# Backward pass of an attention and FFN block: y and dx each in one pass a token tile, 64-row chunks of weight gradients as two column halves

## The chip, the cores and the metric

The kernel runs on one core of one Trainium2 chip. The metric is the device time of one execution in microseconds (us). The kernel before takes 1388.32 us, the median of three runs from 1385.99 to 1391.23.

## The reference

A transformer block with the attention and the FFN side by side, forward and backward in one launch, batch 1, 2048 tokens (S), width 448 (D), 16 heads of 28 (DH), FFN width 1792 (F), all in bf16:

```python
xn = layernorm(x)                                  # no scale, no shift
qkv = xn @ wqkv                                    # [2048, 1344]
p = softmax(q @ k.T * 28 ** -0.5)                  # a head at a time, [2048, 2048]
attn = (p @ v) @ wo
ffn = (silu(xn @ w_gate) * (xn @ w_up)) @ w_down
y = x + attn + ffn
out, vjp = jax.vjp(f, x, wqkv, wo, w_gate, w_up, w_down)
return out, *vjp(grad_out)     # y, dx, dwqkv, dwo, dw_gate, dw_up, dw_down
```

## The kernel before, in words

Token tiles are 128 tokens (16 of them), and the 16 heads go in four groups of four (`g`), two pairs to a group (`hp`). Width 448 is cut into four chunks for gradients whose rows are D (`DCH`): three of 128 rows and one, chunk 3, of 64.

**Forward pass.** For each group of heads the scores of 512 queries by 128 keys are computed, exponentiated and multiplied with V. Between these matmuls PE runs filler units in a fixed order, most of them the FFN: for each of 14 blocks of 128 FFN columns (`fc`) and each of four column chunks of 512 tokens (`sc`) the gate, up and dh products are formed, and `dh_unit` (L422) writes h, da and du for that block side by side into one tile `hda` of 128 x 3 x 512, transposes it by a DMA on the SP queue into `f_sp` (`sp_transpose`, L434 and L435), and stores it whole to DRAM (`F_d`, L436). `dw_unit` (L441) then reads `f_sp` for the weight gradients of this block, 16 matmuls over the token tiles for each of w_down, w_gate and w_up (L445). For the last block the gate and up gradients are not done here: the transposes go to DRAM (`fT_d`, L438) for the backward pass. The attention outputs in transposed form go to `OT_d` (`mid3`, L541 to L543).

**Backward pass.** A loop (L1362) runs over 512 steps k: group, pair of heads, chunk of 512 keys (`kc`), chunk of 512 queries (`qc`), token tile in it (`qi`). In each step:

- `row` (L844): two score matmuls (L852) into PSUM tiles `sb` (3 buffers) and, for the step before, two dP matmuls (L860) into `db` (3 buffers).
- `ew` (L879): two exponentials on ACT (L883), two products on DVE (L891) that give dS; dS is transposed by DMA on SP (L877), except for the last token tile of four, which PE transposes (`tr_unit`, L951, with a copy on ACT, L956). For eleven sets of four steps (`TWO`) PE transposes two tiles.

What follows depends on k mod 4:

- 0: fillers.
- 1: `kv` (L958) adds four steps to the dK and dV accumulator (L969, L973); after 16 steps ACT drains it. The row sums of dx (`aux`) are done here, save where k mod 16 is 1. `dq_unit` (L990) runs 16 matmuls of 256 columns on four column tiles of PE (L1000); ACT drains them (L1004 in the first chunk of keys, else L1013 with an add on POOL, L1015 or L1017).
- 2: fillers.
- 3: fillers, then `tr_unit`.

**Fillers** come from a list, `stream`; each is a generator that issues one matmul at a time and gives its estimated duration in ns. `fill_open` (L1302) takes the next unit, `fill_step` (L1312) issues matmuls until a budget is spent: in steps 2 and 3 of four the budgets are R2 = 560 and R3 = 380 ns; in step 0 what is left of the unit is finished, or, if none is open, a unit of up to 600 ns is opened and run. So one unit normally takes one set of four steps. All use one PSUM tile (`genb`, 1 buffer). In order:

- `late_dw`: the gate and up gradients of the last FFN block, four chunks of 16 matmuls (110 ns each), drained by DVE.
- `y_unit` (L1128): 4 chunks of 512 tokens x 2 halves of the FFN x 4 token tiles, nine matmuls of 448 columns (L1139). Half 0 is added to x by DVE into a float32 tile `yt` (L1144), half 1 is added to that by DVE and stored (L1147). Its operands, `h_c` from `F_d`, `o_c` from `OT_d` and `x_c`, are loaded for half a chunk at a time.
- `dx_open` (L1158): closes the pool of y and opens that of dx.
- `dx_unit` (L1183): three parts of the FFN blocks (`FQ`: 5, 4 and 5 of 14) x 4 chunks of 512 tokens x 4 token tiles; 10, 8 and 10 matmuls (L1195). Part 0 is copied by ACT (L1201) into the float32 array `dxg`, parts 1 and 2 are added to it by DVE (L1203). Operands: `wguT` from the transposed weights, `dau_c` (da and du) from `F_d`.
- `tail_open` (L1210), then `dc_unit` (L1242): the part of dx that comes through q, k and v, eight matmuls a token tile (L1249), an add on DVE, and POOL work on `dxg`.
- As each group of heads ends, eight-transpose units `dsp_unit` and `dsq_unit` and the dwqkv units `dwq_unit` (L1077) are put into the list: four chunks of D rows, 16 matmuls of 336 columns (L1081), four copies (L1088 to L1091) and one store each. `dsq_unit` goes in at the fourth place of the list, `dwq_unit` behind `dx_open` or `tail_open`, at the sixth place or later.

**Loads and stores.** Loads of the backward pass are queued with a due step (`drip`, L785) and issued on SP, some per step, so that each meets its date (`drop`); `have` issues at once what is still held back when its user comes. A store is held for two steps and issued by POOL, after the loop by SP (`store`, `flush`, L842).

**The end.** After step 512 the dx tiles are finished with the last group's q, k and v (`dx_mm`, `dx_a`, `dx_b`, L1358 stores dx), and the last group's `dwq_unit` chunks run with the tag "rest", which makes their copies ACT's.

Of the kernel before, what the change touches and what calls it, by code (L numbers as in the profile page):

```python
# [104 lines left out]
def kernel(  # L105
# [32 lines left out]
    OT_d = dram.tile([4, P, G, 512], BF16)  # L138
    F_d = dram.tile([4, P, NFC, 3, 512], BF16)
    fT_d = dram.tile([P, 4, 2, 4, P], BF16)  # L140
# [144 lines left out]
    def qkv_unit(g, tq, sc, act=False):  # L285
# [12 lines left out]
        else:  # L298
            if tq == 2 and sc == 0:
                if g == 0:  # L300
                    VV[g] = ff.tile([P, 4, 3, 4, P], BF16, name="f_sp")[:, 0:2].rearrange("p a w t f -> p (a w t f)")[:, :S]
# [120 lines left out]
    def dh_unit(fc, sc):  # L422
# [8 lines left out]
        DVE.scalar_tensor_tensor(out=t3[:, 2], in0=ps[:], scalar=0.5, in1=ag[:], op0=ALU.mult, op1=ALU.mult)  # L431
        DVE.scalar_tensor_tensor(out=t3[:, 1], in0=ps[:], scalar=0.5, in1=nn[:], op0=ALU.mult, op1=ALU.mult)  # L432
        if sc == 0:
            fsp[fc] = ff.tile([P, 4, 3, 4, P], BF16, name="f_sp")  # L434
        sp_transpose(fsp[fc][:, sc].rearrange("p w t f -> p (w t) f"), t3[:].rearrange("p w s -> p (w s)"))  # L435
        SP.dma_start(out=F_d[sc, :, fc], in_=t3[:])  # L436
        if fc == NFC - 1 and sc % 2:
            late.append((fT_d[:, sc - 1:sc + 1], fsp[fc][:, sc - 1:sc + 1, 1:3]))  # L438
        yield 216

    def dw_unit(fc, w):  # L441
        rhs = dy_sp if w == 0 else xn_sp
        ps = new_gen([P, 512], FP32, name="gen")
        for t in range(NT):
            PE.matmul(ps[:, :D], lhsT=fsp[fc][:, t // 4, w, t % 4, :], rhs=rhs[:, t, :],  # L445
# [81 lines left out]
    def mid3(g, qc):  # L527
# [14 lines left out]
                     (OT_d[qc, :, g, :], tT[:, 0].rearrange("p q s -> p (q s)")),  # L542
# [210 lines left out]
    yst, wdp = ExitStack(), {}  # L753

    def turn_loads():
# [3 lines left out]
        ye = yst.enter_context(tc.tile_pool(name="ye", bufs=1, side="right", reuse_waits="tile"))  # L759
        wdp[0] = ye.tile([P, 7, D], BF16, name="wd_e")  # L760
# [163 lines left out]
    fT = bk.tile([P, 4, 2, 4, P], BF16, name="dsp", bufs=1)  # L924
# [6 lines left out]
    def late_dw(c):  # L931
        d0, dn = DCH[c]
        ps = ps_g.tile([P, 2, P], FP32, name="genb")
        for t in range(NT):
            PE.matmul(ps[:dn], lhsT=xn_sp[:, t, d0:d0 + dn], rhs=fT[:, t // 4, :, t % 4, :],
                      start=(t == 0), stop=(t == NT - 1))
            if t < NT - 1:
                yield 110
        DVE.tensor_copy(out=w2[:dn, c], in_=ps[:dn])
        for a, o in enumerate((out_4, out_5)):  # L940
            store(o[d0:d0 + dn, F - P:], w2[:dn, c, a])
        yield 110
# [47 lines left out]
    def dq_unit(b):  # L990
# [27 lines left out]
        if qc == 3:  # L1018
# [5 lines left out]
            if hp == 1:  # L1024
                stream[3:3] = [(480, lambda hp=hp: dsq_unit(g, hp)) for hp in range(2)]
# [441 lines left out]
```

## Time and profile before

The profiled execution is one run of its own; the trace and the page are of it.

| | |
|---|---|
| time of the profiled execution | 1388.41 us |
| span of its trace | 1386.6 us |
| mean granted TensorE clock | 0.99 |
| bytes moved by DMA | 266.06 MB, in 664,879 packets |
| packets under 512 bytes | 590,586 |
| ACT exponentials of the backward pass (L883) | 1024, 542.0 us |
| DVE products of the backward pass (L891) | 770 + 254, 484.2 + 163.4 us |
| y matmuls (L1139), dx matmuls (L1195), dwq matmuls (L1081) | 288, 448, 256 |

How to read the profile: PE is TensorE's matmuls, PEld its weight loads, DVE VectorE, ACT ScalarE, POOL GpSimd, SP the sync engine that issues DMAs (SPq is its DMA queue). L12 is line 12 of the kernel. A group of instructions is given as line, engine, operation, out<-in with partitions x elements and type, the count (x16), then busy us, mean ns of one, and idle time before it with what ended it. A row of a window shows its bounds and length, each engine's busy time with its instructions, the granted clock, the mean share of the 16 DMA engines, and GB/s; the count may take in an instruction that lies over a window's edge. The DMA share can go over 1 where packets lie over each other. A row of the timeline shows the start, how long, engine, line, operation, out<-in, and in brackets the idle time before with what ended it; neighbouring instructions of one line are one row. A row of DMA issues gives the count, then least, mean and greatest ns of an issue.

### The profile page before, as it was taken

What the parts mean: (1) busy time and instruction counts of PE and PEld (TensorE: products, weight loads), DVE (VectorE), ACT (ScalarE), POOL (GpSimd) and SP (SyncE); (2) the same over time, 40 slices, a digit from 0 to 9 for tenths busy, and PEclk for the clock granted to TensorE, in tenths of its full rate; (3) what the DMA queues carried; (4) which work ended last, traced back from release to release, by engine and by line L of the source; (5) the groups of instructions that cost most, each with busy time, mean ns of one, the idle gap of its engine ahead of it and who ended that gap; (6) DMA issues with size and microseconds to landing.
All of it is one profiled execution on the core that took longest, in us unless ns stands there. A gap on an engine that the chain in (4) does not pass through costs nothing.

```text
span 1386.6 us, 35026 instructions
## 1 busy us (share of the span) xinstructions
PE 1321.6 (95%) x12808; PEld 563.4 (41%) x12808; DVE 1137.9 (82%) x1996; ACT 1225.6 (88%) x2242; POOL 467.3 (34%) x642
## 2 busy tenths in 40 slices
PE   5899999999999999989999999999999999999997
PEld 2333333333333333334444444444444444444443
DVE  6587666766667676759999999988899999999997
ACT  5799998989999999878899999899889898888995
POOL 6473533463344454301121211201211111114674
PEclk9899999999999999999999999999999999999999
DMA  6697968777788776789999999999999999999992
GB/s 159 150 216 174 232 132 187 180 169 159 169 176 199 161 157 157 170 246 199 219 217 217 222 232 173 213 220 223 249 188 182 196 231 233 206 189 206 209 190 67
DMA packets 664879, 266.06 MB, mean 192 GB/s; under 512 B 590586, under 2 KB 639218, under 8 KB 664706
## 3 DMA queue, kind: packets, MB, share of 16 engines
q1 hardware_dynamic: 656258, 250.59, 89.9%
q0 software_dynamic: 7040, 12.93, 4.1%
q8 instruction: 100, 1.64, 0.5%
q14 instruction: 73, 0.60, 0.1%
q10 hardware_dynamic: 1408, 0.30, 0.1%
HBM read 64.37 MB, written 59.62 MB: 89 GB/s over the span
## 4 chain that ended last, share of the span: by engine, by line
PE 79%; DVE 9%; DMA 4%; ACT 3%; issue 2%; POOL 2%; SPq 0%; ACTq 0%; DVEq 0%; POOLq 0%
PE sb L852 13%; PE acc L969 8%; PE gen L445 8%; PE genb L1195 7%; PE genb L1139 5%; PE s_w L643 4%; PE sb L951 4%; PE sb L1000 4%; PE gen L478 4%; PE gen L380 3%; PE db L860 3%; PE gen L412 3%; PE gen L292 2%; PE gen L426 2%; PE genb L1081 2%
## 5 line engine op out<-in xcount | busy, mean ns | idle before, releaser
L883 ACT ACTIVATE e_sb<-sb 128x512 bf16<-128x512 f32 x1024 | 542.0, 609 | 18.5 <-PE db L860 15.8
L891 DVE TENSOR_TENSOR ds_sb<-db,e_sb 128x512 bf16<-128x512 f32 x770 | 484.2, 682 | 30.7 <-issue 12.2
L646 ACT ACTIVATE eT<-s_w 128x1024 bf16<-128x1024 f32 x256 | 264.5, 1033 | 53.6 <-PE s_ps L643 50.8
L648 ACT ACTIVATE eT<-s_ps 128x512 bf16<-128x512 f32 x512 | 287.1, 614 | 0.0
L852 PE MATMUL sb<-kd,qd 32*128 32x512 bf16 x1024 | 235.2, 381 | 4.3 <-DMA qd<-QD_d 0.9
L860 PE MATMUL db<-kd,qd 32*128 32x512 bf16 x1024 | 230.0, 382 | 3.1 <-DVE ds_sb L891 2.5
L891 DVE TENSOR_TENSOR ds_pe<-db,e_sb 128x512 bf16<-128x512 f32 x254 | 163.4, 685 | 18.7 <-PE db L860 10.2
L1015 POOL TENSOR_TENSOR dq_acc<-dq_acc,dq_st 128x256 f32<-128x256 f32 x64 | 46.1, 720 | 389.7 <-ACT dq_st L1013 389.7
L404 POOL TENSOR_TENSOR nn<-nn,ag 128x512 f32<-128x512 f32 x56 | 71.2, 1271 | 239.6 <-DVE ag L402 238.3
L969 PE MATMUL acc<-e_sb,qd 128*32 128x512 bf16 x1024 | 134.0, 384 | 0.0
L643 PE MATMUL s_ps<-QQ,KK 32*128 32x512 bf16 x512 | 119.1, 387 | 2.2
L1195 PE MATMUL genb<-wguT,dau_c 128*128 128x448 bf16 x448 | 109.8, 356 | 0.0
L973 PE MATMUL acc<-ds_sb,qd 128*32 128x512 bf16 x770 | 106.6, 385 | 0.0
L643 PE MATMUL s_w<-QQ,KK 32*128 32x512 bf16 x512 | 100.6, 389 | 2.2 <-ACT eT L646 0.9
L852 PEld LDWEIGHTS <-qd 32*128 32x128 bf16 x1024 | 48.4, 91 | 127.6 <-issue 109.4
L956 ACT COPY dsT<-sb 128x512 f32<-128x512 f32 x144 | 84.0, 591 | 17.0 <-PE sb L951 8.6
L445 PE MATMUL gen<-xn_t,f_sp 128*128 128x448 bf16 x416 | 91.8, 354 | 0.4 <-DVE nn L419 0.3
L445 PEld LDWEIGHTS <-f_sp 128*128 128x128 bf16 x640 | 55.8, 98 | 76.4 <-issue 28.6
L1000 PE MATMUL sb<-dsT,kd 128*32 128x256 bf16 x2048 | 78.4, 273 | 2.9 <-DMA dsT<-ds_sb 2.9
L951 PE MATMUL sb<-ident_bf,ds_pe 128*128 128x128 bf16 x1016 | 77.6, 219 | 0.3
L951 PEld LDWEIGHTS <-ds_pe 128*128 128x128 bf16 x1016 | 66.1, 98 | 22.4 <-issue 5.5
L478 PE MATMUL gen<-eT,VS 128*32 128x512 bf16 x1024 | 68.6, 382 | 6.2 <-DVE hda L432 2.9
(184 smaller groups left out, 2123.2 us busy)
## 6 DMA issues: line engine op xcount, KB each, us to landing
F_d<-hda SPq DMA_DIRECT2D x56, 384.0 KB
dau_c<-F_d SPq DMA_DIRECT2D x24, 512.0 KB
qd<-QD_d SPq DMA_DIRECT2D x16, 512.0 KB
kd<-KD_d SPq DMA_DIRECT2D x16, 384.0 KB
dsT<-ds_sb SPq DMA_TRANSPOSE x367
h_c<-F_d SPq DMA_DIRECT2D x8, 512.0 KB
wT_d<-wT_f SPq DMA_DIRECT2D x14, 256.0 KB
KD_d<-qk_sp SPq DMA_DIRECT2D x7, 512.0 KB
```

The source lines that it names most:

```text
L445: PE.matmul(ps[:, :D], lhsT=fsp[fc][:, t // 4, w, t % 4, :], rhs=rhs[:, t, :], start=(t == 0), stop=(t == NT - 1))
L643: PE.matmul(sp4[hh], lhsT=KK[g][r:r + HP, kt * P:(kt + 1) * P], rhs=QQ[g][r:r + HP, qsl], start=True, stop=True, tile_position=(r, 0))
L646: ACTE.activation(out=e2[0][:], in_=wide[:], func=ACT.Exp, scale=SCALE)
L648: ACTE.activation(out=e2[1][:, j], in_=sp4[2 + j], func=ACT.Exp, scale=SCALE)
L852: PE.matmul(s_ps[:], lhsT=qside[g, qc][r:r + HP, 0, qi * P:(qi + 1) * P], rhs=kside[g, kc][r:r + HP, 0, :], start=True, stop=True, tile_po ...
L860: PE.matmul(d_ps[:], lhsT=qside[g, qc][r:r + HP, 1, qi * P:(qi + 1) * P], rhs=kside[g, kc][r:r + HP, 1, :], start=True, stop=True, tile_po ...
L883: ACTE.activation(out=est[k][:, j], in_=sps.pop((k, j))[:], func=ACT.Exp, scale=SCALE)
L891: DVE.tensor_tensor(out=ds[:, j], in0=dps.pop((k - 1, j))[:], in1=est[k - 1][:, j], op=ALU.mult)
L951: PE.transpose(ps[:, c, :], ds[:, c // 4, (c % 4) * P:(c % 4 + 1) * P], ident_bf[:])
L969: PE.matmul(a[r:r + HP, :], lhsT=sp4[:, 1, r:r + HP], rhs=e[:, j, :], start=first, stop=last, tile_position=(0, r), skip_group_check=True)
L1000: PE.matmul(ps[r:r + HP, :256], lhsT=ks[:, kt, h:h + HP], rhs=t[:, par::2, j, kt, :], start=(kt == 0), stop=(kt == 3), tile_position=(0, r ...
L1195: PE.matmul(ps[:, :D], lhsT=d[:, i // 2, i % 2, tsl], rhs=dxs["w", fq][:, i // 2, i % 2, :], start=(i == 0), stop=(i == n - 1))
```

## The change

1. **DRAM layout.** `F_d` is replaced by `H_d` (h, in eight chunks of 256 tokens) and `G_d` (da and du of one token tile side by side, in 16 token tiles). `dh_unit` writes da and du interleaved per 128 tokens and issues two stores a tile, where one was. `OT_d` is cut into eight chunks of 256 tokens. The transposed tile `f_sp` and `fT_d` hold the same blocks in the order h, then da and du of each token tile.
2. **y in one pass.** A unit is one token tile: 18 matmuls into one accumulation, one DVE add of x, one store. w_down is held whole, its pool `wr` is later reused for the weights of dx. Loads are per 256 tokens, three sets of buffers.
3. **dx in one pass.** A unit is one token tile: 28 matmuls into one accumulation, one ACT copy into `dxg`. The transposed gate and up weights are held whole, loaded in halves during y and behind `dx_open`; da and du come in three pieces a token tile, five buffers.
4. **64-row chunks.** Chunk 3 of `late_dw` and of `dwq_unit` runs as two halves of the output columns, on PE columns 0 to 63 and 64 to 127: 32 matmuls of half the columns. Its output then lies in 128 partitions: for `dwq_unit` one copy and four stores, where four copies and one store were.
5. **The filler scheduler.** Budgets are 760, 570 and 380 ns in steps 0, 2 and 3; units run over several sets of four steps; a unit is finished when what is left is within the budget and an allowance (230 ns in step 0, 700 for a dwq chunk of 128 rows, none elsewhere); the next one may open at once, but not in step 3 right after a unit ended. `dsq_unit` goes in as soon as the units of 480 ns ahead of it are through, `dwq_unit` behind it. The row sums run in any step 1.

The diff, cut to this:

```diff
@@ forward, dh_unit and dw_unit
-    F_d = dram.tile([4, P, NFC, 3, 512], BF16)
+    H_d = dram.tile([8, P, NFC, 256], BF16)
+    G_d = dram.tile([NT, P, NFC, 2, P], BF16)
...
-        DVE.scalar_tensor_tensor(out=t3[:, 2], in0=ps[:], scalar=0.5, in1=ag[:], op0=ALU.mult, op1=ALU.mult)
-        DVE.scalar_tensor_tensor(out=t3[:, 1], in0=ps[:], scalar=0.5, in1=nn[:], op0=ALU.mult, op1=ALU.mult)
+        t4 = lambda x: x.rearrange("p (t s) -> p t s", s=P)
+        dau = t3[:, 1:3].rearrange("p a s -> p (a s)").rearrange("p (t w s) -> p t w s", t=4, w=2)
+        for w, x in ((1, ag), (0, nn)):
+            DVE.scalar_tensor_tensor(out=dau[:, :, w, :], in0=t4(ps[:]), scalar=0.5, in1=t4(x[:]),
+                                     op0=ALU.mult, op1=ALU.mult)
...
-        sp_transpose(fsp[fc][:, sc].rearrange("p w t f -> p (w t) f"), t3[:].rearrange("p w s -> p (w s)"))
-        SP.dma_start(out=F_d[sc, :, fc], in_=t3[:])
+        sp_transpose(fsp[fc][:, sc], t3[:].rearrange("p w s -> p (w s)"))
+        SP.dma_start(out=H_d[2 * sc:2 * sc + 2, :, fc, :].rearrange("c p s -> p c s"),
+                     in_=t3[:, 0].rearrange("p (c s) -> p c s", c=2))
+        SP.dma_start(out=G_d[4 * sc:4 * sc + 4, :, fc].rearrange("t p w s -> p t (w s)"),
+                     in_=dau.rearrange("p t w s -> p t (w s)"))
@@ dwq_unit
+            r = dsp[g][:, t].rearrange("p k (h r) -> p (k h) r", r=HP)[:, :, :DH]
...
+                for a in range(2):
+                    PE.matmul(ps[64 * a:64 * a + 64, :6 * DH].rearrange("p (a r) -> p a r", r=DH),
+                              lhsT=xn_sp[:, t, d0:], rhs=r[:, 6 * a:6 * a + 6],
+                              start=(t == 0), stop=(t == NT - 1), tile_position=(0, 64 * a), skip_group_check=True)
...
+            cp(out=of[:, :6 * DH], in_=ps[:, :6 * DH])
+            store(w0[:, 0, g * n:(g + 1) * n], of[:64, :n])
+            store(w0[:, 1, g * n:g * n + n // 2], of[:64, n:n + n // 2])
+            store(w0[:, 2, g * n:(g + 1) * n], of[64:, :n])
+            store(w0[:, 1, g * n + n // 2:(g + 1) * n], of[64:, n:n + n // 2])
@@ y_unit
+    def y_unit(t):
+        c = t // 2
+        if t % 2 == 0:
+            have(("y", c, 0))
+            if 0 < c < 6:
+                load_y(c + 2, now + 24)
+            if c > 0:
+                load_w(0, c - 1, c, now + 16)
...
+        for i in range(NFC + G):
+            if i == NH and t % 2 == 0:
+                have(("y", c, 1))
+            l, r = (h_c[:, i, tsl], wd[:, i, :]) if i < NFC else (o_c[:, i - NFC, tsl], wo_sb[:, i - NFC, :])
+            PE.matmul(ps[:, :D], lhsT=l, rhs=r, start=(i == 0), stop=(i == NFC + G - 1))
...
+        DVE.tensor_tensor(out=y[:], in0=ps[:, :D], in1=x_c[:, t % 2, :], op=ALU.add)
+        store(out0_d[:, t, :], y[:])
@@ dx_unit
+    FP = [(0, 5), (5, 10), (10, 14)]
+    def load_dx(n, due):
+        f0, f1 = FP[n % 3]
+        dau[n] = dxs["pool"].tile([P, 5, 2, P], BF16, name="dau")
+        drip(("dx", n), [(dau[n][:, :f1 - f0], G_d[n // 3, :, f0:f1])], due)
+    def dx_unit(t):
...
+            for w in range(2):
+                PE.matmul(ps[:, :D], lhsT=dau[n][:, fc % 5, w, :], rhs=wgu[fc // NH][:, fc % NH, w, :],
+                          start=(fc + w == 0), stop=(fc + w == NFC))
...
+        ACTE.copy(out=dxs["g"][:, t, :], in_=ps[:, :D])
@@ the scheduler
+    R0, R2, R3 = 760, 570, 380
...
+    def fill_step(ns, over=0):
+        nonlocal cur, left, ended
+        if now == ended + 1 and now % 4 == 3:
             return
+        if 0 < left <= ns + over:
+            ns = left + 95
+        n = 0
+        while ns > 95:
+            if cur is None:
+                if n == 0:
+                    fill_open()
+                if cur is None:
+                    return
+            x = next(cur)
+            ns -= x
+            left -= x
+            n += 1
+            if left < 50:
+                run(cur)
+                cur, ended = None, now
...
-            if 9 <= k < NB and cur is None:
-                fill_open(600)
-            fill_step(100 if 18 < k < 36 else BIG)
+            if k == NB:
+                finish()
+                while stream:
+                    run(stream.pop(0)[1]())
+            elif k >= 9:
+                fill_step(100, 0) if k < 36 else fill_step(R0, 700 if whole else 230)
```

More of the change, by code (lines that the diff above doesn't have):

```diff
@@ L1162, in dx_open @@
         dxs["g"] = gp.tile([P, NT, D], FP32, name="dxg")
-        st = dxst.enter_context(tc.tile_pool(name="dxp", bufs=2, reuse_waits="tile"))
-        dxs["pool"] = st
-        load_w(0, now + 15)
-        load_dx(0, 0)
+        dxs["pool"] = dxst.enter_context(tc.tile_pool(name="dxp", bufs=5, reuse_waits="tile"))
+        for n in range(2):
+            load_dx(n, now + 16)
+        for a, b in ((0, 2), (2, 4), (4, 6), (6, 7)):
+            load_w(1, a, b, now + 20 + 2 * a)
+        for n in range(2, 5):
+            load_dx(n, now + 18 + 4 * n)
```

244 lines of the change are left out of this document (105 added, 139 removed).

## Prediction

> **What bounds the kernel now.** I read the page's head first, then the busy time in short stretches of the backward pass, then the order of time inside one of them.
>
> ```profile
> span 1386.6 us, 35026 instructions
> PE 1321.6 (95%) x12808; PEld 563.4 (41%) x12808; DVE 1137.9 (82%) x1996; ACT 1225.6 (88%) x2242; POOL 467.3 (34%) x642
> ```
>
> PE looks like the bound. That is an average over two passes, and matmul ends are modelled, so it decides nothing yet. The change acts in the backward pass, a loop of 512 steps whose pattern repeats every four steps (I call four steps a cycle): four score rows (L852, L860), one block of gradient matmuls (L969, L973, L1000), one set of transposes (L951), and filler matmuls put between them. Stretches that start and end where a cycle starts show its length:
>
> ```profile
> core 0: us, PE busy (x) PEld busy (x) DVE busy (x) ACT busy (x) POOL busy (x), PEclk, DMA share, GB/s
> 655.86:661.40 5.54, 4.79 (x60) 1.96 (x55) 4.97 (x8) 4.78 (x11) 0.72 (x1) 1.00 1.17 202
> 661.40:666.95 5.55, 5.55 (x69) 2.47 (x65) 5.13 (x9) 4.99 (x10) 0.72 (x1) 1.00 1.09 235
> 828.78:839.88 11.10, 11.10 (x134) 4.93 (x130) 10.46 (x19) 10.27 (x21) 0.71 (x1) 1.00 1.09 203
> 862.25:880.44 18.19, 18.19 (x220) 9.37 (x216) 17.23 (x37) 15.29 (x31) 4.01 (x6) 1.00 1.06 230
> 892.81:909.87 17.06, 17.06 (x202) 7.64 (x198) 15.11 (x25) 16.09 (x34) 3.98 (x6) 1.00 1.15 178
> 1040.55:1051.65 11.10, 11.10 (x132) 4.91 (x128) 10.69 (x19) 10.08 (x21) 1.99 (x3) 1.00 0.89 136
> 1125.34:1136.72 11.38, 11.38 (x136) 5.12 (x132) 10.99 (x19) 10.00 (x20) 1.45 (x2) 1.00 1.12 208
> 1319.63:1330.73 11.10, 11.10 (x132) 4.91 (x128) 10.98 (x19) 10.62 (x23) 8.88 (x11) 1.00 1.21 189
> ```
>
> The score-row matmuls of the same stretches count the cycles, eight to a cycle:
>
> ```profile
> 828.78:839.88 11.10, 3.30 (x16) 0.75 (x16) 1.00 1.09 203
> 862.25:880.44 18.19, 5.10 (x24) 1.13 (x24) 1.00 1.06 230
> 892.81:909.87 17.06, 4.95 (x24) 1.13 (x24) 1.00 1.15 178
> ```
>
> So a cycle takes 5.55 us with nine y matmuls as filler (828.78) and 5.55 with eight dx matmuls (1040.55) or eight dc matmuls (1319.63). It takes 5.69 with ten dx matmuls, whether ACT drains them (892.81, 17.06 / 3) or DVE does (1125.34, 11.38 / 2), and 6.06 with a dwq chunk of 16 (862.25, 18.19 / 3). The first two rows are the key: they are neighbours, the first has no filler and no drain at all, the second nine matmuls and one drain on DVE (x9 against x8), and they take 5.54 and 5.55. In the first PE, DVE and ACT are all idle for over half a microsecond. What sets 5.55 is therefore a loop of waits. One cycle in order of time:
>
> ```profile
> 1040.74 0.38 ACT L1013 ACTIVATE dq_st<-sb 128x256 f32<-128x256 f32 x1 [0.42 <-PE sb L1000]
> 1041.02 2.06 ACT L883 ACTIVATE e_sb<-sb 128x512 bf16<-128x512 f32 x4
> 1043.18 0.59 ACT L956 COPY dsT<-sb 128x512 f32<-128x512 f32 x1
> 1043.66 2.07 ACT L883 ACTIVATE e_sb<-sb 128x512 bf16<-128x512 f32 x4
> 1044.13 0.56 PE L852 MATMUL sb<-kd,qd 32*128 32x512 bf16 x2
> 1044.32 0.43 PE L860 MATMUL db<-kd,qd 32*128 32x512 bf16 x2
> 1044.69 0.39 PE L969 MATMUL acc<-e_sb,qd 128*32 128x512 bf16 x2
> 1044.85 0.61 DVE L1203 TENSOR_TENSOR dxg<-genb,dxg 128x448 f32<-128x448 f32 x1
> 1045.56 0.61 PE L1000 MATMUL sb<-dsT,kd 128*32 128x256 bf16 x16
> 1046.11 0.39 PE L852 MATMUL sb<-kd,qd 32*128 32x512 bf16 x2
> 1046.29 0.38 ACT L1013 ACTIVATE dq_st<-sb 128x256 f32<-128x256 f32 x1 [0.55 <-PE sb L1000]
> ```
>
> ACT drains dq, does four exponentials, copies the transposes, and starts the next exponentials at 1043.66. Only the first of those frees the third sb bank, so the L852 pair at 1044.13 takes 0.56 instead of 0.39; L860, L969, L1000 follow in PE's order, and ACT waits 0.55 for that dq. From drain to drain 5.55. The DVE drain (0.61 at 1044.85) lies beside L969 and is in no link. **The floor is 5.55, and only what stands above it can be won.**
>
> **The change part by part**, against the profiled execution's own 1388.41 us (its span is 1386.6; the median of the runs is 1388.32, so no correction).
>
> ```profile
> L1195 PE MATMUL genb<-wguT,dau_c 128*128 128x448 bf16 x448 | 109.8, 356 | 0.0
> L1203 DVE TENSOR_TENSOR dxg<-genb,dxg 128x448 f32<-128x448 f32 x32 | 19.6, 613 | 0.0
> L1147 DVE TENSOR_TENSOR y<-genb,yt 128x448 bf16<-128x448 f32 x16 | 9.8, 613 | 0.0
> L1144 DVE TENSOR_TENSOR yt<-genb,x_c 128x448 f32<-128x448 f32 x16 | 9.8, 613 | 0.0
> ```
>
> *Drains.* y in one pass drops its 16 L1144, dx in one pass its 32 L1203: 9.8 + 19.6 = 29.4 us of DVE go. The 16 ACT copies and 16 L1147 stay. By the two neighbouring rows they are worth 0. If the cover were gone (DVE setting the cycle) the limit would be the PE work of a cycle of nine, below.
>
> [...]
>
> *y, 32 cycles.* 18 matmuls a tile, in the order of instructions of the changed kernel still 3, 2, 4 a cycle: 5.55 before and after, 0.
>
> *dx, 48 cycles.* Same 448 matmuls. Before: 16 tiles of ten, 16 of eight, 16 of ten, one a cycle: 32 x 5.69 + 16 x 5.55 = 270.9. After, 28 a tile go as 9, 9, 10: 16 x (5.55 + 5.55 + 5.69) = 268.6. Term **-2.3**. Bounds: one matmul in a run of five costs
>
> ```profile
> 918.68 1.12 PE L1195 MATMUL genb<-wguT,dau_c 128*128 128x448 bf16 x5
> ```
>
> (1.12 - 0.36) / 4 = 0.19, so a cycle of nine could be 5.69 - 0.19 = 5.50 and dx 267.0 (-3.9; y would give -1.6 more). If nine cost as much as ten, +2.2.
>
> *dwq chunk 3.* A 64-row chunk ran 16 matmuls of 336 columns; now 32 of 168 in two column halves. That two halves run abreast is not in the trace, but four column tiles do: the 16 L1000 of 256 columns take 0.55 from 1045.56 to the next row, 0.034 each, far under what the chunk's own matmuls show one after another:
>
> ```profile
> 1365.19 2.46 PE L1081 MATMUL genb<-dsp,xn_t 128*128 128x336 bf16 x16
> ```
>
> That is 0.154 for 336 columns, so some 0.117 for 256. 32 halves at the L1000 rate take 32 x 0.034 = 1.1 us, one after another 32 x 0.077 = 2.5. I take the former, which the tiles shown do; then the cycle falls from 6.06 to the floor: 0.5 x 3 groups, **-1.5**; bounds -2.0 and 0. late_dw's chunk 3 sits in light cycles: 0, bounds -0.5 and +0.5.
>
> *Order.* dsq and dwq come up to two cycles earlier, the row sums may run in every cycle; their number is unchanged: 0, bounds -1 and +1.
>
> *Forward.* F_d's one store a tile becomes H_d (two 512-byte pieces a row) and G_d (four): 768 pieces for 128 of 3072 bytes, and one more issue on SP.
>
> ```profile
> q1 hardware_dynamic: 656258, 250.59, 89.9%
> 300.00:450.00 150.00, 141.17 (x1026) 53.50 (x1027) 101.05 (x176) 136.13 (x213) 63.91 (x86) 1.00 0.81 178
> ```
>
> ```profile
> L436 SPq DMA_DIRECT2D F_d<-hda x56: 415/584/1210, 75.8 to 588.5; - x56
> ```
>
> ```profile
>   DMA f_sp<-hda: 12.3, 6
> ```
>
> The mean packet costs 0.899 x 1386.6 x 16 / 656258 = 30 ns on an engine, so 640 more cost at most 1.2 us of all 16 engines a tile; from below nothing, since the bytes are the same. A tile comes every 512.7 / 55 = 9.3 us and DMA is 0.81 busy. The next thing behind such a store is the next tile's transpose into f_sp, for which PE and its weight loads already wait 12.3 us in six places. I take **+1.5**; bounds 0 and +14 (the slower rival). The extra issue (0.58) stands on SP, which waits for tiles anyway.
>
> [...]
>
> *Loads.* h comes in runs of 3.5 KB a row instead of 1 KB, dau in 2 to 2.5 KB instead of 2. Same bytes. One place can show it:
>
> ```profile
> 992.22 0.62 PE L1000 MATMUL sb<-dsT,kd 128*32 128x256 bf16 x16 [1.19 <-DMA dsT<-ds_sb]
> ```
>
> Where a group of heads begins, loads and stores crowd and PE waits 1.19 for a transpose. The changed kernel issues a little less there at the second and third change of group and more at the first (one chunk of y further ahead). I take **-1.0**, bounds -4 and +3.
>
> *Tail.* The last dwq chunk 3 is off the path, but its one store becomes four, on SP ahead of the last two output stores:
>
> ```profile
> 1381.58 0.56 SPq L842 DMA_DIRECT2D out_dram<-dwq_o  x1
> 1383.23 0.81 SPq L1358 DMA_DIRECT2D out_dram<-ds_sb  x2
> ```
>
> 1381.58 + 4 x 0.56 = 1383.82 against 1383.23: **+0.6**, bounds 0 and +1.5.
>
> *Column changes.* Every fourth cycle drains a finished dk/dv accumulator as well, and costs more beside ten matmuls than beside nine:
>
> ```profile
> 839.88:845.53 5.65, 5.65 (x69) 2.51 (x65) 5.50 (x10) 5.29 (x11) 0.72 (x1) 1.00 1.06 161
> 909.87:915.79 5.92, 5.92 (x70) 2.61 (x66) 5.14 (x9) 5.80 (x12) 0.00 (x0) 1.00 1.17 290
> ```
>
> 0.10 over 5.55 with nine (y), 0.23 over 5.69 with ten. Of 12 such dx cycles 8 had ten, some 4 will: 4 x 0.13 = **-0.5**, bounds -1 and 0.
>
> **Sum:** -2.3 - 1.5 + 1.5 - 1.0 + 0.6 - 0.5 = -3.2, 1388.4 - 3.2 = **1385.2**; by the bounds of the terms, not all at one end together, 1380 to 1389.
>
> **Rivals.** *The freed 29.4 us count.* If DVE set the cycle where nine or more matmuls drain on it, y and dx would go to 5.50 (-1.6 and -1.6 beyond the sum), the change of columns would cost nothing (-1), and the crowding at the changes of group would go too (-3 beyond): 1378, range 1374 to 1381. For: DVE is busy 10.99 of 11.38 and 10.98 of 11.10. Against: the empty cycle of 5.54. *The change does nothing it says:* halves run one after another (+1.5), nine cost what ten cost (+4.5 beyond): 1391. Against: the 828.78 row. *Slower:* the 512-byte stores hold the next transposes back in the forward pass. It decides where f_sp lands after the first matmul of the weight-gradient unit that reads it; three stalls are over that edge now. If each of the 14 column blocks waits one more microsecond, +14: 1398, range 1393 to 1404. For: 0.81 busy, and 1.2 us more in 9.3. Against: the transposes have most of a tile's time to land.
>
> **How the numbers follow.** The forecast 0.40 (0.10 of it below 1381.4), drains count 0.32, does nothing 0.07, slower 0.21 (0.02 of it under 1395.3). Half a per cent, 6.9 us, is about what a measurement of this kernel can tell from no change: faster 0.10 + 0.32 = 0.42, within it 0.30 + 0.07 + 0.02 = 0.39, slower 0.19. Cases of both signs hold much, so the forecast's own range is 1380 to 1389; the range for 8 in 10 takes in most of the first rival's and the near end of the slower one: 1375 to 1395.
>
> **What would show it.** In the trace of the changed kernel a cycle of y should still be 5.55, dx 5.55, 5.55, 5.69, the cycle of dwq chunk 3 5.55 to 5.65, and DVE idle some 0.5 us more in a cycle without a drain, beside the same 0.5 of ACT waiting for L1000. dx cycles of 5.50 would mean that the loop is not the floor; below that the whole reading is wrong. The forward pass should end within 2 us of where it did; idle of PE before f_sp well over 12.3 would be the slower rival. A y cycle over 5.6 with DVE idle would mean that a drain was doing something useful.

## The result and the profile after

The changed kernel takes 1386.42 us (median of 22 runs, 1381.20 to 1392.19), the kernel before, beside it, 1390.20 (22 runs, 1385.99 to 1397.97). The ratio is 0.9967 with a 95% interval of 0.9955 to 0.9979: a gain of 4.6 us (2.9 to 6.3), where 3.2 was forecast; the two medians lie 3.8 apart. The profiled execution took 1384.51 us, 3.9 less than that of before. The head of its page:

```profile
span 1382.7 us, 35269 instructions
PE 1316.1 (95%) x12888; PEld 560.6 (41%) x12888; DVE 1113.1 (81%) x1939; ACT 1225.9 (89%) x2239; POOL 471.9 (34%) x651
```

DVE lost 24.8 us of work and the span 3.9. The cycles that answer to those of the prediction, as windows of the changed kernel (first two cycles of y; then three of dx with nine, nine and ten matmuls; then chunk 3 of dwq, of the first and of the third group; last two cycles of dc, the first of them with row sums beside the drain of a finished accumulator):

```profile
831.76:842.86 11.10, 11.10 (x134) 4.92 (x131) 10.49 (x18) 10.28 (x21) 0.93 (x2) 1.00 1.25 203
895.08:911.86 16.78, 16.78 (x200) 7.47 (x197) 14.99 (x25) 15.39 (x32) 3.99 (x6) 1.00 1.12 245
883.36:889.08 5.72, 5.72 (x92) 2.96 (x88) 5.20 (x10) 5.18 (x11) 1.38 (x2) 1.00 1.23 184
1239.33:1244.91 5.58, 5.55 (x92) 2.95 (x89) 5.21 (x10) 4.90 (x10) 1.38 (x2) 1.00 1.26 215
1279.54:1285.74 6.20, 5.87 (x68) 2.54 (x65) 5.59 (x10) 6.20 (x15) 3.76 (x5) 1.00 1.31 201
1285.74:1291.29 5.55, 5.55 (x68) 2.43 (x65) 5.50 (x10) 5.39 (x13) 3.76 (x5) 1.00 1.06 216
```

y is 5.55 a cycle with one DVE instruction less in two cycles (x18 against x19), dx 16.78 / 3 = 5.59, that is 5.55, 5.55 and 5.68, and chunk 3 takes 5.72 and 5.58 where these two took 6.37 and 6.16. So the y and dx cycles are what was forecast to a few hundredths, and chunk 3 to 0.07. The dc cycle of 6.20 was not forecast: the row sums now fall beside a drain. Cutting the trace into passes gives another picture. The weight loads of the score row of step 9 (first of the two lines) and of step 511, before:

```profile
L852 PEld LDWEIGHTS <-qd x2: 91/91/91, 618.6 to 618.6; 32*128 32x128 bf16 x2
L852 PEld LDWEIGHTS <-qd x3: 90/91/93, 1347.8 to 1347.8; 32*128 32x128 bf16 x3
```

and after:

```profile
L857 PEld LDWEIGHTS <-qd x2: 91/91/91, 621.9 to 621.9; 32*128 32x128 bf16 x2
L857 PEld LDWEIGHTS <-qd x3: 90/91/94, 1342.9 to 1342.9; 32*128 32x128 bf16 x3
```

Up to step 9 the changed kernel is 3.3 us later, from there to step 511 it is 721.0 against 729.2, 8.2 shorter, and from step 511 to the end of the span 39.8 against 38.8, 1.0 longer: +3.3 - 8.2 + 1.0 = -3.9. The forecast had +1.5, -5.3 and +0.6. Two rows of the page (first before, then after) show where the backward pass gained more than the cycles tell:

```profile
L1000 PE MATMUL sb<-dsT,kd 128*32 128x256 bf16 x2048 | 78.4, 273 | 2.9 <-DMA dsT<-ds_sb 2.9
```

```profile
L1011 PE MATMUL sb<-dsT,kd 128*32 128x256 bf16 x2048 | 78.3, 273 | 0.0
```

PE no longer waits for a transposed dS. And the forward pass lost, most of it at one place. PE and its weight loads wait 13.3 us for f_sp in eight places, against 12.3 in six before; that is not the "well over 12.3" that the prediction named as the sign of the slower rival. In the timeline after, the matmul that waits longest for f_sp:

```profile
309.73 0.36 PE L452 MATMUL gen<-dy_t,f_sp 128*128 128x448 bf16 x1 [3.42 <-DMA f_sp<-hda]
```

The window behind it (the granted clock is the third number from the end):

```profile
309.70:315.00 5.30, 5.27 (x22) 1.80 (x23) 2.50 (x5) 2.55 (x4) 0.96 (x2) 0.68 1.02 155
```

and behind the same stall (3.06 us) before:

```profile
308.60:314.00 5.40, 5.33 (x32) 2.10 (x33) 3.93 (x7) 4.24 (x7) 2.10 (x3) 1.00 1.22 190
```

In about the same time PE ran 22 matmuls instead of 32: the stall ended about 1 us later than before's, and a stretch at half clock behind it (granted 0.50 from 310.7 to 313.7) brings the lag to 2.7 us. At the end of the kernel, in the timeline of SP, the four stores of the last chunk 3 take 2.42 us on SP ahead of the last output stores:

```profile
1376.69 2.42 SPq L847 DMA_DIRECT2D out_dram<-dwq_o  x4
1379.21 1.00 SPq L1391 DMA_DIRECT2D out_dram<-ds_sb  x2
```

### The profile page after: what moved, and what is told of

The parts are those of the page before. It is cut to its first block, busy times and chain, and to the rows that moved or that the text cites. A ratio compares the mean times of both kernels' runs of the same rounds, so it can differ in the third digit from the quotient of the medians.

```text
span 1382.7 us, 35269 instructions
## 1 busy us (share of the span) xinstructions
PE 1316.1 (95%) x12888; PEld 560.6 (41%) x12888; DVE 1113.1 (81%) x1939; ACT 1225.9 (89%) x2239; POOL 471.9 (34%) x651
## 4 chain that ended last, share of the span: by engine, by line
PE 80%; DVE 9%; ACT 3%; DMA 3%; issue 3%; POOL 1%; SPq 0%; ACTq 0%; DVEq 0%; POOLq 0%
PE sb L857 13%; PE acc L980 9%; PE gen L452 8%; PE genb L1215 7%; PE genb L1172 5%; PE s_w L650 4%; PE sb L962 4%; PE gen L485 4%; PE sb L1011 4%; PE gen L381 3%; PE db L865 3%; PE gen L413 3%; PE gen L427 2%; PE gen L293 2%; PE genb L1266 2%
## 5 line engine op out<-in xcount | busy, mean ns | idle before, releaser
L980 PE MATMUL acc<-e_sb,qd 128*32 128x512 bf16 x1024 | 134.0, 384 | 0.0
L1215 PE MATMUL genb<-w,dau 128*128 128x448 bf16 x448 | 109.8, 356 | 0.0
L1011 PE MATMUL sb<-dsT,kd 128*32 128x256 bf16 x2048 | 78.3, 273 | 0.0
```

The lines of the kernel that those rows point to most:

```text
L980: PE.matmul(a[r:r + HP, :], lhsT=sp4[:, 1, r:r + HP], rhs=e[:, j, :], start=first, stop=last, tile_position=(0, r), skip_group_check=True)
L1011: PE.matmul(ps[r:r + HP, :256], lhsT=ks[:, kt, h:h + HP], rhs=t[:, par::2, j, kt, :], start=(kt == 0), stop=(kt == 3), tile_position=(0, r ...
L1215: PE.matmul(ps[:, :D], lhsT=dau[n][:, fc % 5, w, :], rhs=wgu[fc // NH][:, fc % NH, w, :], start=(fc + w == 0), stop=(fc + w == NFC))
```

## The experiments

Each is an edit of the changed kernel unless it says otherwise. Theory: a loop of waits sets 5.55 a cycle, the drains lie beside it, and what is won is the tenth dx matmul, chunk 3 and waits for DMA. Rival: the drains were the gain. The 95% intervals of the ratios are 0.0012 to 0.0029 to each side (1.7 to 4 us), and most of them overlap, so a term of 1 to 3 us is read from the cycles of one profiled execution of each kernel, not from the times.

**The drains put back.**

```diff
+            if i == 8:
+                yt = yp.tile([P, D], FP32, name="yt", bufs=2)
+                DVE.tensor_tensor(out=yt[:], in0=ps[:, :D], in1=x_c[:, t % 2, :], op=ALU.add)
+                ps = ps_g.tile([P, 512], FP32, name="genb")
...
+                if 2 * fc + w == 17:
+                    DVE.tensor_tensor(out=dxs["g"][:, t, :], in0=ps[:, :D], in1=dxs["g"][:, t, :], op=ALU.add)
```

> The changed kernel with the drains of before put back: y is closed after nine matmuls and added to x into a float32 tile, dx after 9 and 18, with the two DVE adds of before; order and number of the matmuls are those of the changed kernel. The floor theory (a loop of waits between PE and ACT, and PE's own work, set a cycle; DVE has room): y cycles stay 5.55, dx cycles 5.55, 5.55, 5.69; DVE busy goes from 1113 back to about 1142, and the time stays within 1.5 us of the changed kernel's 1386.4. The rival (fewer drains are the gain): cycles of 5.60 to 5.65 wherever a drain comes back, 48 cycles, so 4 to 8 us more, 1390 to 1394.

Measured 1387.47 (12 runs), ratio to before 0.9974 (0.9957 to 0.9990). Its y window, and 25 cycles of dx from steps 290 to 390, then the same 25 of the changed kernel:

```profile
826.30:837.40 11.10, 11.10 (x134) 4.92 (x131) 10.98 (x19) 9.99 (x20) 0.56 (x1) 1.00 1.14 221
1029.22:1171.18 141.96, 141.80 (x1666) 63.57 (x1662) 133.08 (x218) 131.52 (x266) 24.50 (x38) 1.00 1.14 211
```

```profile
1028.27:1169.64 141.37, 141.21 (x1666) 63.28 (x1662) 126.48 (x203) 130.90 (x265) 24.45 (x38) 1.00 1.12 208
```

With 6.6 us more of DVE work the stretch is 0.59 longer; y is unchanged. From step 9 to 511 it takes 723.7 against 721.0, 2.6 longer, of which 0.93 and 0.78 are two cycles with late dS transposes (steps 70 and 262) and -0.7 are row sums that fell elsewhere. The rest, 1.6 us, is dx's: of the 16 middle cycles of a tile, twelve are 0.10 to 0.26 longer and four are not. They stand behind ACT's copy of dx, which this edit moves from the cycle of ten matmuls to the first cycle of nine, and the time is lost in their score pairs, ahead of the DVE add. At step 202 the first score pair of the changed kernel, then of this one:

```profile
900.64 0.39 PE L857 MATMUL sb<-kd,qd 32*128 32x512 bf16 x2
900.72 0.50 PE L857 MATMUL sb<-kd,qd 32*128 32x512 bf16 x2
```

So no cycle of y or dx got longer by a DVE add that came back; that the place of ACT's copy is what costs the 1.6 is read from the timelines, not tested. The rival's own price was put down too high: 48 cycles of 0.05 to 0.10 make 2.4 to 4.8, not 4 to 8. The sum of 2.6 alone would not refute it; the cycles do.

**dx as 10, 8, 10.** Budgets of step 0 chosen so that a tile goes as before's three parts did, in one pass.

```diff
-                fill_step(100, 0) if k < 36 else fill_step(R0, 700 if whole else 230)
+                fill_step(100, 0) if k < 36 else fill_step({23 * 189: 950, 13 * 189: 570}.get(left, R0) if isdx else R0, 700 if whole else 230)
```

> The changed kernel with the 28 matmuls of a dx tile put as 10, 8, 10 over three cycles instead of 9, 9, 10; one pass and one drain stay. Theory (ten matmuls stand 0.14 above the floor, nine and eight stand on it): 16 cycles go from 5.55 to 5.69, +2.2, and some cycles of a column change by 0.13 more, +0 to +0.5: 1388.6 to 1389.2. Rival (the dx cycles got shorter because the DVE adds went): no change, 1386.4.

Measured 1387.80, ratio 0.9981 (0.9967 to 0.9996). The same 25 cycles:

```profile
1029.13:1171.73 142.60, 142.44 (x1666) 64.01 (x1662) 126.69 (x203) 130.21 (x265) 24.49 (x38) 1.00 1.14 207
```

1.23 longer than the changed kernel's with the same matmuls and drains; from step 9 to 511 it is 2.4 longer, as the forecast's 16 x 0.14 = 2.2 has it.

**Chunk 3 whole.** Both units with before's 16 matmuls, copies and one store.

```diff
-            if dn == P:
...
+            PE.matmul(ps[:dn].rearrange("p (a r) -> p a r", r=DH), lhsT=xn_sp[:, t, d0:d0 + dn], rhs=r,
+                      start=(t == 0), stop=(t == NT - 1))
```

> The changed kernel with chunk 3 of the weight gradients whole again (16 matmuls of 64 rows, four copies and one store). Theory (two halves run abreast, and a cycle with the whole chunk stands above the floor): the three cycles of chunk 3 go from 5.65 on average back to 6.1 or more, +1.3 to +2; the end after step 511 loses the three extra stores, -0.6 to -1; sum +0.5 to +1.5, 1387 to 1388. Rival (halves run one after another): cycles unchanged, the time 0.5 to 1 shorter by the end.

Measured 1387.40, ratio 0.9977 (0.9963 to 0.9991). The third group's chunk, which takes 5.58 in halves:

```profile
1242.18:1248.34 6.16, 6.16 (x76) 3.21 (x73) 5.65 (x13) 5.00 (x10) 1.38 (x2) 1.00 1.11 258
```

The three cycles are 0.64, 0.51 and 0.58 longer, and the end after step 511 is 38.9 instead of 39.8. The halves do run abreast: the 32 of the first group keep PE busy 1.73 us in the changed kernel, where before's 16 whole matmuls of this chunk keep it 2.8. Their four stores cost 0.9 once. (From step 9 to 511 this execution took 4.0 longer. Another 1.6 of that lie in the cycle of step 206, where PE waits for a load of dx weights, and 0.6 in others.)

**One store a tile in the forward pass.**

```diff
-        SP.dma_start(out=H_d[2 * sc:2 * sc + 2, :, fc, :].rearrange("c p s -> p c s"),
-                     in_=t3[:, 0].rearrange("p (c s) -> p c s", c=2))
-        SP.dma_start(out=G_d[4 * sc:4 * sc + 4, :, fc].rearrange("t p w s -> p t (w s)"),
-                     in_=dau.rearrange("p t w s -> p t (w s)"))
+        SP.dma_start(out=F_d[sc, :, fc], in_=t3[:].rearrange("p w s -> p (w s)"))
```

> The changed kernel with one store a tile in the forward pass again, rows of 3072 bytes as before; the backward pass then reads h and da, du in pieces of 512 bytes instead of 2 to 3.5 KB. In the profiled pair the forward pass of the changed kernel ended 3.2 us later than before (row of step 9 at 621.9 against 618.6), a stall on f_sp that grew from 3.06 to 3.42 and a stretch of half clock behind it. Theory: the second issue on SP and the smaller pieces cause this, so the row of step 9 comes back to 618 to 619.5, f_sp idle to about 12, and the time falls by 2 to 3 to 1383.5 to 1384.5 if the smaller loads are hidden. Rival one: the forward difference is variation between executions; the row of step 9 stays between 620 and 623 and the time at 1386. Rival two: the 512-byte loads hold dS transposes back in the backward pass, idle of PE before the dq matmuls rises from 0 to 2 or more and eats the gain.

Measured 1386.62, ratio 0.9970 (0.9951 to 0.9988): no gain in sum beside the changed kernel. The score row of step 9:

```profile
L853 PEld LDWEIGHTS <-qd x2: 90/90/91, 619.2 to 619.2; 32*128 32x128 bf16 x2
```

The dq matmuls, of its page:

```profile
L1007 PE MATMUL sb<-dsT,kd 128*32 128x256 bf16 x2048 | 78.4, 273 | 4.1 <-DMA dsT<-ds_sb 4.1
```

The forward pass is 2.7 shorter than the changed kernel's, and the backward pass, which now loads in 512-byte pieces, 5.4 longer: 4.1 of waits for dS and what hangs on them. The second rival is right. Between the theory and the first rival, variation between executions, this run does not decide: the same forward pass ended anywhere from 618.7 to 623.1 in eight executions (below, under Forward).

**Later attention stores.** They wait until the next f_sp transpose is issued; and the row sums keep off the steps with k mod 16 = 1.

```diff
-                     (OT_d[2 * qc:2 * qc + 2, :, g, :].rearrange("c p s -> p c s"), tT[:, 0].rearrange("p (c q) s -> p c (q s)", c=2)),
-                     (QD_d[g, qc, :, 1, :], tT[:, 1].rearrange("p q s -> p (q s)")))
+        late_od.extend([(OT_d[2 * qc:2 * qc + 2, :, g, :].rearrange("c p s -> p c s"), tT[:, 0].rearrange("p (c q) s -> p c (q s)", c=2)),
+                        (QD_d[g, qc, :, 1, :], tT[:, 1].rearrange("p q s -> p (q s)"))])
...
-            while aux and aux[0][0] <= k:
+            while aux and aux[0][0] <= k and (k % 16 != 1 or k >= NB):
```

> The changed kernel with two edits that lie in different passes. Forward: the stores of the transposed attention output wait until the next f_sp transpose has been issued, so that SP does not stand still for the odT transpose in front of it (the transpose that PE waits for at 309 in the changed kernel was issued at 305.1, while its source was ready near 300). Backward: the row sums are kept off steps with k mod 16 = 1 again. Theory: the f_sp transpose starts about 3 us earlier, the 3.4 us stall goes to under 1, the half-clock stretch behind it goes, and the row of step 9 comes 4 to 6 us earlier than 621.8; the row sums give back 0.6 near the end; the time falls by 4 to 6, to 1380.5 to 1382.5. Rival (the transpose is late because the DMA engines are busy, not because of SP's order): it starts earlier but lands when it did, the forward pass ends at 620.5 to 622.

Measured 1384.34, ratio 0.9958 (0.9939 to 0.9977), span 1378.1. The timeline of SP and PE at the place (the changed kernel issued this transpose at 305.07):

```profile
302.44 2.72 SPq L204 DMA_TRANSPOSE f_sp<-hda  x1
...
307.98 0.36 PE L454 MATMUL gen<-dy_t,f_sp 128*128 128x448 bf16 x1 [2.37 <-DMA f_sp<-hda]
```

The window behind it:

```profile
308.00:313.00 5.00, 4.95 (x29) 1.87 (x30) 2.35 (x4) 3.93 (x7) 2.63 (x6) 1.00 1.12 163
```

The score row of step 9:

```profile
L859 PEld LDWEIGHTS <-qd x2: 90/90/91, 618.1 to 618.1; 32*128 32x128 bf16 x2
```

Issued 2.6 earlier it lands 1.75 earlier; the stall is 2.37, the clock stays at 1.00, and the pass ends 3.8 earlier, with the same pieces and stores. So SP's order sets part of it; that busy DMA engines set the rest is not tested. In eight executions with the changed kernel's own order PE went on at 308.8 to 312.0 here, so 307.98 is outside that spread; the end of the pass, 618.1 against their 618.7 to 623.1, only just is. The dc cycles sum to 90.90 instead of 91.74.

**Stores on POOL.** `SP.dma_start` of the two stores becomes `POOL.dma_start`.

> The changed kernel with the two stores of a tile (h, and da with du) issued by POOL instead of SP. Theory (the extra issue on SP's queue is what costs the forward pass 2.4 to 3 us): SP has two issues a tile less, the row of step 9 is at 618 to 619.5, f_sp idle under 12, and the time falls by 2 to 4. Rival one (the 640 extra pieces themselves hold the transposes back): no change, 621 to 622. Rival two (POOL's issues delay its own steps of the gate chain, 112 issues of 0.6 us and more): forward later than 622.

Measured 1406.49, ratio 1.0113 (1.0086 to 1.0140); step 9 at 639.3. POOL's issues in the forward pass (least, mean and greatest ns, first and last start):

```profile
L440 POOL DMA_DIRECT2D H_d<-hda x56: 710/758/774, 66.4 to 604.6; - x56
L442 POOL DMA_DIRECT2D G_d<-hda x56: 767/773/795, 67.2 to 606.9; - x56
```

The idle time before users of f_sp (us, times):

```profile
  DMA f_sp<-hda: 25.8, 5
```

That is rival two: POOL spends 0.76 or 0.77 us on each of 112 issues and waits 24.6 us for hda before them, and the forward pass ends 17.5 us later.

**What the loop consists of.** Four kernels: four sb and two db banks; dq drained by DVE instead of ACT; 2 of the 18 matmuls of a y tile, so that y leaves out most of its sum; and the last two together.

```diff
-                s_ps = ps_b.tile([P, 512], FP32, name="sb", bufs=3)
+                s_ps = ps_b.tile([P, 512], FP32, name="sb", bufs=4)
```

> The changed kernel with four PSUM buffers for sb and two for db instead of three and three. Theory (the floor of 5.55 us comes from three sb banks: the last score row of a cycle must wait for the first exponential behind the transposes): with a fourth bank that row does not wait, cycles with nine fillers go to PE's own 5.50 and those with eight to 5.3 to 5.4, so the backward pass loses 4 to 8 us unless two db banks take over. Rival one (two db banks decide: the dP row then waits for the DVE product before it): cycles longer than 5.55, the time 5 us or more above. Rival two (the floor has nothing to do with sb): 5.55 as before.

Measured 1518.77, ratio 1.0931 (1.0904 to 1.0957). A dP row:

```profile
843.63 0.37 PE L865 MATMUL db<-kd,qd 32*128 32x512 bf16 x1
844.23 0.37 PE L865 MATMUL db<-kd,qd 32*128 32x512 bf16 x1 [0.23 <-DVE ds_sb L896]
```

In its timeline the second matmul of the pair waits for DVE to free a bank. Over the pass such waits are 54 us in 240 places, against 2.0 in four in the changed kernel. Two db banks decide, so this says nothing on the sb link.

```diff
-        st = bk.tile([P, 256], FP32, name="dq_st", bufs=1)
-        ACTE.mul(out=st[:], in_=ps[:, :256], mul=SCALE)
+        if kc < 3:
+            DVE.scalar_tensor_tensor(out=dq_acc[:, qsl], in0=ps[:, :256], scalar=SCALE, in1=dq_acc[:, qsl],
+                                     op0=ALU.mult, op1=ALU.add)
+            return
```

> The changed kernel with all dq results drained by DVE (scaled and added to dq_acc there) instead of ACT and POOL. Theory as recorded in the prediction (ACT's drain of dq is a link of the loop): ACT loses 0.38 a cycle, cycles with nine fillers go to 5.50, those with eight or with few to 5.3 to 5.45; the backward pass loses 3 to 8 us. Rival (the drain lies beside the loop, which goes from the first exponential over the score row, L980, L1011 and the next score row to the exponentials; two cycles in which the kernels already drain on DVE take 5.55): 5.55 stays, the time within 2 us; cycles with two tiles transposed by PE may get 0.1 to 0.3 shorter, since ACT has a second copy there.

Measured 1388.22, ratio 0.9981 (0.9963 to 0.9998). Two dc cycles of it, and of the changed kernel:

```profile
1293.79:1305.37 11.58, 11.43 (x132) 4.77 (x129) 11.46 (x21) 10.29 (x23) 7.53 (x9) 1.00 1.18 202
```

```profile
1291.29:1302.39 11.10, 11.10 (x132) 4.85 (x129) 10.99 (x19) 10.78 (x25) 8.21 (x10) 1.00 1.13 193
```

Taking 0.38 off ACT wins nothing; beside another DVE drain it costs 0.24 a cycle, since DVE is then full (11.46 of 11.58). From step 9 to 511 this run takes 2.1 more than the changed kernel.

```diff
+            if i in (0, NFC + G - 1):
+                PE.matmul(ps[:, :D], lhsT=l, rhs=r, start=(i == 0), stop=(i == NFC + G - 1))
```

> The changed kernel with 2 of the 18 matmuls of a y tile, so y leaves out most of its sum; drains, loads and all else stay. It shows the floor itself over the 32 y cycles. Theory (a loop of waits sets 5.55, PE's work does not): y cycles stay at 5.5 to 5.55 though 16 of 18 matmuls are gone. Rival (PE's work sets the cycle): they fall by the matmuls gone, 8 x 0.19, to 4.8 at most 5.0.

One execution: 1395.51. Two of its y cycles:

```profile
742.24:747.78 5.54, 5.19 (x61) 1.98 (x57) 5.49 (x9) 4.79 (x10) 0.21 (x1) 1.00 1.18 208
699.24:706.24 7.00, 6.86 (x61) 2.35 (x57) 4.96 (x8) 5.58 (x11) 1.22 (x2) 0.74 1.10 247
```

Where the clock is full, a cycle without eight of nine matmuls takes 5.54: PE's work does not set the floor. What neither theory had: 11 of the 32 y cycles take 6.74 to 7.20, at a granted clock of 0.74 to 0.84.

> The kernel of the run with light y (2 of 18 matmuls, y incomplete) with dq drained by DVE in all cycles. With PE far from full it shows whether ACT's drain of dq is a link of the loop. If it is (the prediction's reading), a cycle loses up to 0.38 and takes 5.2 to 5.3. If it lies beside the loop, as the run with dq on DVE suggests, cycles without another DVE drain stay at 5.5 to 5.55 and those with y's DVE add take 5.7 to 5.8.

One execution: 1393.33. A cycle with y's DVE add:

```profile
736.98:742.49 5.51, 5.19 (x61) 1.97 (x57) 5.38 (x11) 4.52 (x9) 0.34 (x1) 1.00 1.09 195
```

With this 13 of the y cycles take 5.51 or 5.52; the light kernel itself has three of 5.51, and its others without more work take 5.54 or 5.55. So a cycle is at most 0.04 shorter, not 0.3: the time of ACT's drain of dq is no link of the loop. The sb bank of dq still has to be drained, now by DVE, so this does not show that the bank is no link. Seven cycles run at 0.74 to 0.83 here.

**Before once more.**

> The kernel before, a second profiled execution. In the first one PE stood still for 3.06 us at 305.6 and the granted clock stayed at 1.00 behind it, while stalls of 2.66 to 3.45 at the same place were followed by half clock in six of the other kernels' traces, and one of 2.37 was not. If the clock depends on chance as well as on length, this look may show the half clock (row of step 9 near 620 to 621 instead of 618.6), and then up to 2 us of the forward loss that the pair of profiles shows is no effect of the change. If it stays at 1.00 and 618.6, the loss of 3.2 belongs to the change. The backward pass should repeat its waits for dS transposes near steps 262 and 386 to 394.

1393.77, 5.4 above the first execution. In its timeline the same stall, and a wait for dS at step 386:

```profile
308.90 0.46 PE L445 MATMUL gen<-dy_t,f_sp 128*128 128x448 bf16 x1 [3.13 <-DMA f_sp<-hda]
...
1176.25 1.05 PE L1000 MATMUL sb<-dsT,kd 128*32 128x256 bf16 x16 [3.12 <-DMA dsT<-ds_sb]
```

The window behind the stall, and that of the cycle without fillers (5.54 in the first execution):

```profile
308.90:314.00 5.10, 4.88 (x20) 1.74 (x22) 2.40 (x4) 2.44 (x4) 0.82 (x2) 0.67 0.90 191
656.60:663.70 7.10, 6.35 (x60) 2.28 (x56) 4.99 (x9) 5.09 (x11) 0.72 (x1) 0.78 1.09 183
```

So the half clock of the forward pass is not the change's: before has it too, in the second of its two profiled executions (0.67 behind the stall). The waits for dS in front of the dq matmuls are before's: 2.9 us in the first execution, 3.3 in this one; 0 to 0.3 in nine kernels with the new layout, 0.9 with the stores on POOL, 1.3 with the drains back, and 4.1 with one store and 512-byte loads.

**All together.** This kernel has the later stores (QD_d from od too), the row sums off k mod 16 = 1, dq on DVE between `dx_open` and `tail_open` only, and the last group's chunk 3 whole.

> The changed kernel with five edits: the two of the run with later attention-output stores (f_sp transposes ahead of OT_d and QD_d, row sums off steps with k mod 16 = 1); the third attention store, QD_d from od, goes behind the f_sp transpose too; dq is drained by DVE between dx_open and tail_open only, where a cycle has no other DVE drain; the last group's chunk 3 runs whole, with one store. By the traces so far: forward row of step 9 at 617 to 618 (618.1 with later stores alone), dx cycles of a change of columns 0.1 shorter, -1 to -2 in the backward pass, the end 0.9 shorter; span 1374.5 to 1376.5 against 1382.7 of the changed kernel and 1378.1 of the run with later stores. If DVE drains of dq lengthen cycles here as they do beside y and dc (+0.24), it comes out at 1378 or more.

Measured 1380.85 (6 runs), ratio 0.9920 (0.9892 to 0.9949), span 1377.5: the fastest, though short of the expectation. From step 9 to 511 it took 718.8 against 720.1 of the run with later stores, as expected; the forward pass ended at 619.6, 1.6 later than there. Its interval is the only one that lies wholly below that of the changed kernel. Its timeline:

```profile
300.97 2.07 SPq L204 DMA_TRANSPOSE f_sp<-hda  x1
...
307.66 0.36 PE L454 MATMUL gen<-dy_t,f_sp 128*128 128x448 bf16 x1 [2.86 <-DMA f_sp<-hda]
```

The window behind the stall:

```profile
307.70:313.00 5.30, 5.08 (x21) 1.84 (x23) 2.58 (x5) 2.62 (x4) 1.09 (x4) 0.68 1.41 218
```

Issued another 1.5 earlier, f_sp landed 0.3 earlier. From here SP's order gains little, which fits busy DMA engines (a share of 1.41 in this window) but was not tested. The half clock is back.

## Why the prediction was right, and where it was not

The time and its sign came out, with the likeliest case; two of its terms were off by more than 1.5 us in opposite directions. In the table the cycles of a kind are summed from score row to score row in the two profiled executions.

| term | forecast | pair of profiles | by experiment |
|---|---|---|---|
| dx, tenth matmul | -2.3 | 16 tens fewer x 0.14 = -2.2 | +2.4 when put back |
| drains and y | 0 | y 182.90 to 182.61: -0.3 | +1.6 when put back, in dx |
| dwq chunk 3 | -1.5 | dwq 73.27 to 71.81: -1.5 | +1.7 when whole |
| order, row sums | 0 (-1 to +1) | dc 91.24 to 91.74: +0.5 | -0.8 when undone |
| forward stores | +1.5 (0 to +14) | +3.3 | not settled: -2.7 with one store, within the spread |
| loads and column changes | -1.5 | the rest, -4.7 | +5.4 with 512-byte loads |
| tail | +0.6 | +1.0 | -0.9 with one store |

**Drains.** The key step, the two neighbouring cycles with and without a drain, held for what it compares: a drain on DVE. It says nothing of ACT's copy, whose place in a dx tile goes with the 1.6 us of the run that puts the drains back. By the first rival the 29.4 us of DVE would have counted; no y or dx cycle of that run is longer by a DVE add.

**The floor.** Its size was right, its working partly wrong. The step that says "ACT drains dq" names a link that is none: in the light kernel the cycle is 5.51 without it and 5.51 to 5.55 with it. The row that seemed to prove it (ACT waits 0.55 for L1000) shows that ACT waits for dq, not that the cycle waits for ACT's drain. What stays, from the first exponential behind the dS copy over the score row, L980, L1011 and the next score row back to the exponentials, is read from the timeline; its sb bank is not tested, since the attempt ran into db.

**Loads.** The term was mis-sized: -1.5 with the column changes, against -4.7 in the pair. The forecast took the one wait of 1.19 at step 262 for its size. Before also loses time to late dS at steps 386 to 394, and waits 3.12 there in its second execution. In the run with one store only the pieces of the layout changed, at 512 bytes, and the waits came back (4.1), so the length of the pieces counts. That before's own pieces of 1 and 2 KB cause its waits is not tested: the changed kernel also loads at other steps. Nor does the pair settle the size, since before's second execution took 733.5 us from step 9 to 511 against 729.2.

**Forward.** The place was right, f_sp behind the stores; the price is not settled. Eight executions run the same forward pass, since their edits lie in the backward pass: the changed kernel, the drains put back, chunk 3 whole, dx as 10, 8, 10, four sb banks, dq on DVE, and the two light kernels. Their step 9 stands at 618.7 (light y), 620.0, 621.0, 621.1, 621.7, 621.8, 621.9 and 623.1, and that of before at 618.6 and 619.6. The means are 2.0 apart, single pairs -0.9 to 4.5. Of the pair's 3.3, 1.6 are the half clock (the lag is 1.1 where the stall ends and 2.7 behind it), which the first execution of before and light y escaped and the second of before did not. That before's first profile was one of the shorter runs (1388.41 against a median of 1390.2) agrees. The run with one store, at 619.2, lies within the spread, so its 2.7 is no measured price. What lies beyond the spread is that PE went on at 307.98 behind the stall in the run with later stores, where the eight did at 308.8 to 312.0.

So what the stores in 512-byte pieces cost was not shown. As loads, 512-byte pieces cost 5.4 against runs of 2 to 3.5 KB, in one execution each.

The total was nearer than its terms: in the pair of profiles the forward loss was 1.8 larger than forecast and the loads' gain 3.2 larger. That they nearly offset each other is luck.

## What to carry to other kernels

Before counting an engine's saved work as time, find two neighbouring stretches with and without it: a busy share of 90% said nothing here, and two equal cycles said what a DVE drain costs, though not what ACT's copy does. Before reading a difference of some us from one pair of profiles, compare executions that share the code of that stretch: the same forward pass varied by 4.4 us here. A layout in DRAM can have a price at the store and one at the load (here 512-byte loads went with a backward pass 5.4 us longer, and the store's price is not settled); look at which of them stands in front of a transfer that the critical engine waits for. Fill work that costs nothing may still pay: with most of y's matmuls left out, eleven and seven cycles of the two light kernels ran at a granted clock of 0.74 to 0.84, each in one execution; that the missing work is the cause was not tested.

## What the runs showed of the hardware

The half clock was not tied to the length of a stall alone. At the stall near 306 us it followed idle times of PE of 2.66 to 3.51 in ten executions (granted 0.67 to 0.68 in the windows behind it of the changed kernel, all together and before's second execution), failed to follow 3.06 (before) and 3.09 (light y), and did not follow 2.37 (later stores; 1.00 in the windows of these three). So it came behind 2.66 in one execution and not behind 3.09 in another; what decides was not shown.

Nor was a stall needed at all: eleven cycles of the light kernel, with 61 matmuls instead of 69, ran at 0.74 to 0.84 and took about 7 us, though PE shows 6.86 of 7.00 busy in one of them and its longest idle time from step 9 to 511 is 0.50. So did seven cycles of the second light kernel and one cycle without fillers of before (0.78). Others with 61 matmuls kept 1.00 (5.54 us); what sets the clock in these cycles was not shown.
